# Gate and up of a gated MLP by Strassen's scheme in 11 of 14 groups, on one core

## The chip, the cores and the metric

The kernel runs on one core of a Trainium2 chip. The metric is the device time of one execution in microseconds. A run is one such time; the time before is the median of three runs. The profile is of one execution, and its span (first to last instruction) is a little shorter than a run. The engines are TensorE (PE, with its weight loads PEld), VectorE (DVE), ScalarE (ACT), GpSimd (POOL) and SyncE (SP), which issues nearly all DMAs.

## The reference

One transformer block on 2048 tokens of width 448, in float32. The first half is layer norm, 16 heads of sliding-window attention (window 256) and a residual sum. The second half is what the change is about:

```
g = layernorm(h) @ w_gate        # (2048 x 448) @ (448 x 1792)
u = layernorm(h) @ w_up          # the same shape
out = h + (gelu(g) * u) @ w_down # (2048 x 1792) @ (1792 x 448)
```

## The kernel before, in words

**Numbers.** Every large float32 operand is split in two parts of a shorter format, `hi` (rounded, on ACT, `to_hi` L352) and `lo` (the rest, mostly on DVE, `to_lo` L355). A product is hi·hi + hi·lo + lo·hi, three matmuls.

**Attention.** It runs in 16 blocks (four chunks of 512 tokens by four groups of heads). PE makes projections (L630), values (L578), scores (L680), probabilities (L755), attention sums (L793) and the output projection (L851); DVE takes the row maxima (L684), ACT the exponentials (L759), POOL the masks (L774). Layer norms are in `layer_norms` and `normalise`; those of the second half are transposed by DVE (L443) and through DRAM (L447 to L457) into `xT`.

**Feed-forward.** F = 1792 is cut into 14 tiles of 128 columns, held in groups of 3, 4, 4 and 3 (`GROUPS`); for each group the four chunks of 512 tokens are gone through. A product (`product`, L1011) is one tile by one chunk, gate and up: 56 products. K = 448 is three and a half times 128 rows. The first four products are made with full-height matmuls (L1024), 11 for gate and 11 for up. The other 52 are *paired* (`pair`, L996): the array is used as two halves of 64 rows, and gate runs in one half while up runs in the other; a second phase swaps the halves. The phases have 10 and 11 pairs of 64x512 matmuls. Between them a one-element ACT read of the bank (`seen`, L1004) makes sure that one half's writes are done before the other half writes the same bank. After a product ACT makes the gelu (L1064), DVE the product (L1066), ACT and DVE the split (L353, L356), and the down projection follows two products later: four phases of pairs of 64x448 matmuls a product, in two *down halves* of six pairs. When a group of tiles is through for a chunk, DVE adds the four banks to the residual `hres` (L1102).

**Order.** Nothing is scheduled by the compiler. The kernel records its operations with a cost, a key and their dependencies; `Lists.run` (L133) builds a fixed list for each engine from them, always taking the operation with the lowest key among those that could start first. The feed-forward's paired phases and down halves are chained one behind the other (end of `feed_forward`, L948), in the order phase, down half, phase, down half. Engines run their lists in order. Banks 0 to 3 serve gate and up, 4 to 7 down.

**Weights.** One load per tile (`weight_load`), split on ACT and DVE (`weight_splits`, the first two tiles on POOL), into seven places that are used in turn.

Of the kernel before, what the change touches and what calls it, by code (L numbers as in the profile page):

```python
# [16 lines left out]
NT = S // 128  # L17
# [7 lines left out]
GROUPS = [3, 4, 4, 3]  # L25
REC = 2944
# [8 lines left out]
LAG_T = 5.0  # L35
FETCH = 180
VLAST = (-30, -25, 14, 24)
ELAST = 2
WKEY = (256, 271)
LAG_P = 15.5  # L40
LAG_V = 9.5
EDGE = 7
WIN = 10
FFN = 1000
LEAD = 20
MARGIN = 0.7
START = 0.8
EARLY = 2
SWAP = -60
HOLDO = 1  # L50
AHEAD = 7
BEHIND = 5
LN1 = (0, -18, 55, 128)
LN2 = (158, 233)
VKEY = (-30, -23, 14, 24)
# [4 lines left out]
PAIRED = 4  # L60
TURNED = (12, 13, 14, 15)
SPANS = {"pp", "proj", "raw", "xT", "h", "rqf", "rkf", "vm", "rec0", "rec1", "rec2", "gh"}
# [167 lines left out]
def block_kernel(ctx: ExitStack, tc, x, wqk_in, wv_in, wo_in, ffn_in, out):  # L230
# [16 lines left out]
    rq_m = pool.tile([128, 4096], F32R, name="rq")  # L247
    rk_m = pool.tile([128, 6144], F32R, name="rk")
# [3 lines left out]
    mt = pool.tile([128, 768], F32, name="mt")  # L252
    xn = [pool.tile([128, D], F32, name=f"xn{i}") for i in range(2)]
# [19 lines left out]
    ffn_d = dram.tile([128, 1472], F32, name="ffn2")  # L273
    xn_d = [dram.tile([D, 128], F32, name=f"xn{t}") for t in range(NT)]
# [3 lines left out]
    fst = ExitStack()  # L278
    lp = fst.enter_context(tc.tile_pool(name="late", bufs=1))
    pp_m = lp.tile([128, 4 * PPB * 128], F32, name="pp")  # L280
# [4 lines left out]
    rec = []  # L285

    def open_rec():
        fst.close()
        p = ctx.enter_context(tc.tile_pool(name="fp", bufs=1))
        rec.extend(p.tile([128, REC], F32R, name=f"rec{i}") for i in range(2))  # L290
        rec.append(p.tile([128, S], F32R, name="xh"))
        rec.append(p.tile([128, 1024], F32R, name="gh"))


    rq = [rq_m[:, 2048 * u:2048 * u + 2048].rearrange("p (j t) -> p j t", j=4) for u in range(2)]
    rk = [rk_m[:, 3072 * u:3072 * u + 3072].rearrange("p (j t) -> p j t", j=4) for u in range(2)]
# [4 lines left out]
    ge = mt[:, 0:512]  # L301
# [39 lines left out]

    def at_v(t):
        return 7 - t % 8
# [14 lines left out]
    def dma(key, size, fn, r=(), w=(), cost=0.44, after=()):  # L358
        return op("sp", cost, 0, key, fn, r, w, size=size, after=after)
# [37 lines left out]
    def normalise(t, key, kind):  # L397
        moved = kind == "ln2" or t in TURNED
        i2, i4 = 0 if moved else t % 2, t % 4
        b = None if moved else Bank(kind)  # L400

        def norm():
            nc.scalar.activation(xn[i2], hres[:, t, :], AF.Identity, scale=bnve[:, 1, i4:i4 + 1],  # L403
                                 bias=bnve[:, 2, i4:i4 + 1])
# [20 lines left out]
        if kind == "ln1" and t in POOLED:  # L425
            op("pool", 1.0, 1.1, key, norm_pool, [HR(t), ("bnve", i4)], [("xn", i2)], port=True)
        else:
            op("act", 0.7, 0.76, key, norm, [HR(t), ("bnve", i4)], [("xn", i2)])
        if moved:
            turn(t, key, kind)  # L430
            turned(t, key, kind)
            return
        op("pe", 0.44, 0.61, key, tr, [("xn", i2), "ident"], (), b)
# [6 lines left out]
    def turn(t, key, kind):  # L440
        d = xn_d[t]
        xb, at = (v_m[:, 0:D], span("vm", 0, D)) if kind == "ln2" and t > 11 and t % 2 else (xn[1], ("xn", 1))
        op("dve", 0.56, 0.65, key, lambda: nc.vector.transpose(xb, xn[0]), [("xn", 0)], [at], port=True)  # L443
        for a in range(4):
            dst = d.rearrange("(b i) t -> i b t", i=32)[:, :, 32 * a:32 * a + 32]
            src = xb[32 * a:32 * a + 32].rearrange("i (b t) -> i b t", t=32)
            dma(key, 150, lambda dst=dst, src=src: nc.sync.dma_start(dst, src), [at], [("xnd", t, a)])  # L447

    def turned(t, key, kind):
        tc = t if kind == "ln2" else col(t)  # L450
# [830 lines left out]
```

## Time and profile before

| | us |
|---|---|
| runs: median (lowest to highest) | 719.81 (719.48 to 720.09) |
| span of the profiled execution | 718.0 |
| PE busy / PEld busy | 710.8 / 592.1 |
| DVE / ACT / POOL busy | 396.8 / 349.1 / 163.4 |

The page gives the span, not a time of its own for the profiled execution; the span is 1.8 us below the median of the runs. Attention fills the first 300 us or so, and the feed-forward runs from there to the end. In rows of groups, `out<-in` are tile names, then partitions x elements, count, busy us and mean ns of one, and the idle time before them with what ended it. Rows of a timeline have start, duration, engine, line, operation and tiles. A PE row's duration reaches to the modelled end of its last matmul, so rows overlap; pitches are read from starts.

### The profile page before, as it was taken

What the parts mean: (1) busy time and instruction counts of PE and PEld (TensorE: products, weight loads), DVE (VectorE), ACT (ScalarE), POOL (GpSimd) and SP (SyncE); (2) the same over time, 40 slices, a digit from 0 to 9 for tenths busy, and PEclk for the clock granted to TensorE, in tenths of its full rate; (3) what the DMA queues carried; (4) which work ended last, traced back from release to release, by engine and by line L of the source; (5) the groups of instructions that cost most, each with busy time, mean ns of one, the idle gap of its engine ahead of it and who ended that gap; (6) DMA issues with size and microseconds to landing.
All of it is one profiled execution on the core that took longest, in us unless ns stands there. A gap on an engine that the chain in (4) does not pass through costs nothing.

```text
span 718.0 us, 14862 instructions
## 1 busy us (share of the span) xinstructions
PE 710.8 (99%) x5716; PEld 592.1 (82%) x5716; DVE 396.8 (55%) x1034; ACT 349.1 (49%) x787; POOL 163.4 (23%) x284
## 2 busy tenths in 40 slices
PE   8999999999999999999999999999999999999997
PEld 7887778788878887778888888888888888888886
DVE  7957688988788789857544312335132235132224
ACT  7738676768667679875533222244222223222221
POOL 5604553644454466541000000000000000000000
PEclk9999999999999999999999999999999999999999
DMA  8895976787858787223641000021000000001002
GB/s 312 265 309 177 279 190 178 198 255 204 221 131 239 202 255 180 64 77 73 188 136 43 1 2 1 1 84 55 33 1 2 1 1 1 2 1 52 22 32 103
DMA packets 96926, 82.03 MB, mean 114 GB/s; under 512 B 41736, under 2 KB 83016, under 8 KB 96840
## 3 DMA queue, kind: packets, MB, share of 16 engines
q1 hardware_dynamic: 96712, 80.98, 39.5%
q8 instruction: 45, 0.74, 0.4%
q14 instruction: 25, 0.20, 0.1%
q10 hardware_dynamic: 144, 0.11, 0.0%
HBM read 50.27 MB, written 31.03 MB: 113 GB/s over the span
## 4 chain that ended last, share of the span: by engine, by line
PE 94%; ACT 2%; DVE 2%; POOL 1%; issue 1%; DMA 0%; DVEq 0%; ACTq 0%
PE bank L1000 52%; PE bank L630 10%; PE bank L755 7%; PE bank L680 6%; PE bank L793 6%; PE bank L578 5%; PE bank L851 4%; PE bank L1024 3%; PE bank L408 1%; ACT rq L353 1%; ACT xn L403 0%; DMA hres<-in_x_dram 0%; DVE hres L854 0%; DVE hres L1102 0%; PE bank L711 0%
## 5 line engine op out<-in xcount | busy, mean ns | idle before, releaser
L684 DVE CUSTOM_DVE_ANT_0 mt<-bank,mt 128x384 bf16<-128x384 f32 (+2 forms) x256 | 127.5, 527 | 33.9 <-PE bank L680 31.0
L1066 DVE TENSOR_TENSOR mt<-bank,mt 128x512 f32<-128x512 f32 x54 | 37.1, 688 | 142.2 <-ACT mt L1064 142.2
L759 ACT ACTIVATE pp<-bank 128x384 f32<-128x384 f32 (+1 forms) x212 | 103.2, 533 | 22.5 <-PE bank L755 18.3
L630 PE MATMUL bank<-xT 128*128 128x512 f32 x308 | 94.6, 397 | 0.0
L774 POOL TENSOR_SCALAR_AFFINE_SELECT pp<-pp 128x512 f32<-128x512 f32 x120 | 75.0, 640 | 67.0 <-ACT pp L759 62.7
L1064 ACT ACTIVATE mt<-bank 128x512 f32<-128x512 f32 x54 | 32.2, 596 | 117.1 <-PE bank L1000 117.1
L1000 PE MATMUL bank<-xT,rk 64*128 64x512 f32 x656 | 82.0, 388 | 0.0
L1000 PE MATMUL bank<-xT,rec 64*128 64x512 f32 x656 | 82.0, 388 | 0.0
L755 PE MATMUL bank<-rq,rk 104*128 104x384 f32 (+2 forms) x352 | 81.4, 305 | 0.4 <-ACT pp L759 0.3
L680 PE MATMUL bank<-rk,rq 84*128 84x384 f32 (+2 forms) x256 | 80.6, 340 | 0.0
L1102 DVE TENSOR_TENSOR hres<-bank,hres 128x448 f32<-128x448 f32 (+1 forms) x65 | 35.7, 611 | 67.8 <-PE bank L1000 66.0
L1000 PEld LDWEIGHTS bank<-xT,rec 64*128 64x128 f32 x656 | 63.0, 184 | 12.2
L1000 PEld LDWEIGHTS bank<-xT,rk 64*128 64x128 f32 x656 | 63.0, 184 | 12.2
L755 PEld LDWEIGHTS bank<-rq,rk 104*128 104x128 f32 x352 | 59.1, 189 | 13.7 <-ACT pp L759 3.8
L1000 PE MATMUL bank<-xT,proj 64*128 64x512 f32 x533 | 66.9, 389 | 0.4 <-ACT e L1006 0.3
L1006 ACT ACTIVATE e<-bank 1x1 f32<-1x1 f32 x162 | 25.7, 159 | 79.4 <-PE bank L1000 78.8
L630 PEld LDWEIGHTS bank<-xT 128*128 128x128 f32 x308 | 55.6, 189 | 6.2 <-ACT xT L353 0.2
L1000 PEld LDWEIGHTS bank<-xT,proj 64*128 64x128 f32 x533 | 51.0, 184 | 11.0 <-ACT e L1006 1.1
L680 PEld LDWEIGHTS bank<-rk,rq 84*128 84x128 f32 x256 | 46.8, 189 | 11.7 <-DVE mx L684 1.7
L353 ACT ACTIVATE rq<-bank 8x512 fp32r<-8x512 f32 x64 | 37.7, 589 | 27.9 <-PE bank L711 26.9
L578 PE MATMUL bank<-proj,xT 128*128 128x448 f32 (+1 forms) x220 | 47.5, 334 | 0.0
L793 PE MATMUL bank<-pp,v 128*29 128x384 f32 (+2 forms) x704 | 45.4, 388 | 0.0
(147 smaller groups left out, 1075.1 us busy)
## 6 DMA issues: line engine op xcount, KB each, us to landing
rk<-k SPq DMA_DIRECT2D x44, 336.0 KB
rq<-q SPq DMA_DIRECT2D x32, 336.0 KB
v<-in_ffn_dram SPq DMA_DIRECT2D x7, 736.0 KB
q<-proj SPq DMA_DIRECT2D x11, 448.0 KB
raw<-in_ffn_dram SPq DMA_DIRECT2D x6, 736.0 KB
xn<-xn SPq DMA_DIRECT2D x72, 56.0 KB
xT<-xn SPq DMA_DIRECT2D x20, 192.0 KB
hres<-in_x_dram SPq DMA_DIRECT2D x16, 224.0 KB
```

The lines of the kernel that those rows point to most:

```text
L353: nc.scalar.activation(dst, src, AF.Copy)
L578: op("pe", mm(224 * n), 0.29 if n == 1 else 0.38, key + a / 16, lambda a=a, h=h, wb=wb, xb=xb: nc.tensor.matmul(bank[b.k][:, 0:224 * n], x ...
L630: op("pe", mm(512) + 0.002, 0.403, key, lambda a=a, h=h, wb=wb, xb=xb: nc.tensor.matmul(bank[b.k], wqk[m][:, h, wb, :], xT[:, xb, cc * 128 ...
L680: nc.tensor.matmul(bank[b.k][:, o:384], rq[u][0:3 * DH, j, i * 128:i * 128 + 128], rk[u][0:3 * DH, j, m0 * 128:(i + 3) * 128], start=True, ...
L684: nc.vector.tensor_tensor_reduce(junk[s % 2][:, o:384], bank[b.k][:, o:384], mask[:, o:384], 1.0, -BIG, OP.add, OP.max, mx[:, i, j:j + 1])
L755: nc.tensor.matmul(bank[b.k][:, n * i:n * i + n], rk[u][0:104, j + i, m * 128:m * 128 + 128], rq[u][0:104, j + i, lo * 128:(hi + 1) * 128] ...
L759: nc.scalar.activation(pp[:, j:j + G, o * 128:o * 128 + n], bank[b.k][:, 0:G * n].rearrange("p (g t) -> p g t", g=G), AF.Exp, scale=SCALE)
L774: nc.gpsimd.affine_select(a, a, pattern=[[0, 4], [-cm, 128]], compare_op=op_, fill=0.0, base=0, channel_multiplier=cm)
L793: nc.tensor.matmul(bank[b.k][32 * j:32 * j + DH + 1, lo * 128:(hi + 1) * 128], v[:, at_v(4 * c - 2 + m), 4 * g + j, :], pp[:, j, at[m] * 1 ...
L1000: nc.tensor.matmul(bank[bk.k][:, 0:n], w, m, start=bool(start), stop=bool(stop), tile_position=(64 * x, 0), skip_group_check=True)
L1066: op("dve", 0.605, 0.702, key + 2 * NP, lambda: nc.vector.tensor_tensor(blocks(g2), src(1), blocks(g2), op=OP.mult), [*G2, *held[1]], G2, ...
L1102: nc.vector.tensor_tensor(hres[:, t, c0:c0 + w], bank[b.k][:, c0:c0 + w], hres[:, t, c0:c0 + w], op=OP.add),
```

## The change

The 14 tiles become 7 pairs of tiles and the four chunks 2 pairs of chunks: 14 groups of 256 columns by 1024 tokens, each gate and up. The order is pairs 0 to 4 with the first chunk pair, 5 and 6 with both, then 0 to 4 with the second (`ORDER2`).

- **Strassen, 11 groups.** 384 of the 448 rows are taken as two halves of 192 = 3 x 64. Columns, rows and tokens in two halves each make a 2x2 block product, done with seven products instead of eight (Winograd's form: sums of weight blocks and of token blocks are made first, and partial results are shared). The 64 rows left are added in the ordinary way. A *unit* is gate or up of a group. A *slot* is two things on the two halves of the array, three terms each: three pairs of 64x512 matmuls. Two units share 25 slots; a down half stands after every third one and at the seams, eight in all.
- **Reads in between.** Products 1, 6, 7 and 4 accumulate in one bank. After product 1 and after product 6 ACT copies the bank (`copied`), after product 7 DVE adds it to a partial result (`added`), and then the next product goes on in the same bank. A second bank is read once on its way, and a third at its end.
- **New operations.** POOL makes the weight sums (6 a weight set), DVE mostly the token sums (4 for each of three row blocks and chunk pair), ACT and DVE split both. Weights go from the input to DRAM scratch (`bounce`) and from there to SBUF, 64 rows at a time, into three buffers. Weights of pairs 3 and 4 and so on are loaded for each chunk pair where they are not used back to back.
- **First three groups, ordinary.** Pairs 0, 1, 2 with the first chunk pair are made as before in 64-row pairs (`cslot`), 28 slots a group. Group 0's operations are placed among the last blocks of attention. The full-height matmuls are gone. Layer norms of tokens 1024 to 2047 come later.
- **Last down group.** Group 13's down weights have places of their own, and its first chunk uses the banks of gate and up.
- `xn` and `v` space, banks and keys are rearranged for this; constants of the planner (`LAG_T`, `LN1`, `VKEY` and others) are set anew.

Core of the diff, with the paired product replaced:

```diff
-GROUPS = [3, 4, 4, 3]
+CL = 3
...
-    def pair(key, n, lat, a, b, r, banks):
-        def go():
-            for x, (bk, w, m, start, stop) in enumerate((a(), b())):
-                nc.tensor.matmul(bank[bk.k][:, 0:n], w, m, start=bool(start), stop=bool(stop),
-                                 tile_position=(64 * x, 0), skip_group_check=True)
-        return op("pe", mm(n), lat, key, go, r, (), banks)
...
+    PRODUCT = {1: (0, 0), 6: (0, 1), 7: (0, 2), 4: (0, 3), 2: (1, 0), 5: (1, 1), 3: (1, 2)}
...
+        order = (5, "22", 2, "11", 3, "12")
+        u.long = [(p, k, u.a) for p in (1, 6, 7, 4) for k in range(3)] + [("21", 0, u.a)]
+        u.short = []
+        for p, rest in zip(order[::2], order[1::2]):
+            b = u.b if p == 2 else u.c
+            u.short += [(p, k, b) for k in range(3)] + [(rest, 0, b)]
...
+    def both(key, *two):
...
+            for t, (wl, xl) in enumerate(((0, 0), (0, 1), (1, 0))):
+                for u, p, k, b, (side, ws, wk, xs, xk) in two:
+                    w = rest_at(wl) if ws == 4 else warea(u.w, wl, ws, side, wk, 1)
+                    nc.tensor.matmul(bank[b.k], w, xarea(u.cp, xl, xs, side)[:, xk], start=p in (1, 2, 5) and not k and not t,
+                                     stop=t == 2, tile_position=(64 * side, 0), skip_group_check=True)
+        queued(op("pe", 0.69, 0.86, key, go, reads, (), [x[3] for x in two]))
...
+    def after(key, u, p, k):
+        last = k == 2
+        if p == 1 and last:
+            copied(key, u.buf["11"], u.a)
+        elif p == 6 and last:
+            copied(key, u.buf["12"], u.a)
+        elif p == 7 and last:
+            added(key, u.buf["22"], u.a)
+            finished(key, u, "22")
+        elif p == "21":
+            finished(key, u, "21")
+        elif p == "22":
+            copied(key, u.buf["22"], u.c)
+        elif p == "11":
+            added(key, u.buf["11"], u.b)
+            finished(key, u, "11")
+        elif p == "12":
+            added(key, u.buf["12"], u.c)
+            finished(key, u, "12")
...
+            for i in range(12):
+                key = start + UNIT * i / 12.5
+                if i in (3, 6, 9):
+                    pause(key)
+                slot(key, (ua, *ua.long[i]), (ua, *ua.short[i]))
+            key = start + UNIT
+            seen(key, ua.a)
+            pause(key)
+            slot(key, (ua, *ua.long[12]), (ub, *ub.long[0]))
```

`pause` places the next waiting down half; `queued` chains a PE operation behind the one before. `weight_set` holds the weight sums, for example:

```diff
+        sum_(0, SE, 2, lambda: at(0, 1, 2), lambda: at(0, 2, 2), OP.add, wtok(n, 0, 1, 2) + wtok(n, 0, 2, 2))
+        sum_(384, SG, 2, lambda: at(0, 0, 2), lambda: at(0, 1, 2), OP.subtract, wtok(n, 0, 0, 2) + wtok(n, 0, 1, 2))
```

950 lines of the change are left out of this document (669 added, 281 removed).

## The prediction, made before the changed kernel ran

> **What bounds the kernel now.** I read the page first, for the share of TensorE and for the chain that ended last.
>
> ```profile
> span 718.0 us, 14862 instructions
> ...
> PE 710.8 (99%) x5716; PEld 592.1 (82%) x5716; DVE 396.8 (55%) x1034; ACT 349.1 (49%) x787; POOL 163.4 (23%) x284
> ...
> PE 94%; ACT 2%; DVE 2%; POOL 1%; issue 1%; DMA 0%; DVEq 0%; ACTq 0%
> ```
>
> TensorE (PE) is busy for 99% and makes 94% of the chain. A busy PE need not be a full one, so I looked next at stretches of the run, at the waits, and at the matmul pitch inside one product.
>
> ```profile
> 300.00:325.00 25.00, 24.93 (x172) 19.17 (x172) 14.56 (x28) 20.33 (x40) 8.17 (x12) 1.00 0.30 73
> 325.00:350.00 25.00, 24.74 (x216) 20.26 (x215) 16.55 (x33) 11.60 (x29) 3.21 (x8) 1.00 0.53 119
> 400.00:700.00 300.00, 300.00 (x2744) 256.96 (x2742) 92.24 (x148) 79.95 (x229) 0.00 (x0) 1.00 0.05 17
> ```
>
> The columns are the stretch, its length, busy time of PE, PEld, DVE, ACT and POOL, granted clock, DMA share and GB/s. From 400 to 700 us PE has no gap at clock 1.00, while DVE works 31% of the time, ACT 27% and POOL not at all. In the list of waits, PE's on the feed-forward's bank reads come to one row:
>
> ```profile
> PE bank L1000 <- ACT e L1006: 0.3, 1, 0.3
> ```
>
> (total, times, longest, in us). Then the pitch, from the timeline:
>
> ```profile
> 401.74 2.67 PE L1000 MATMUL bank<-xT,rk 64*128 64x512 f32 x21
> ...
> 404.03 0.39 PE L1000 MATMUL bank<-xh,rk 64*128 64x512 f32 x1
> ...
> 404.25 1.37 PE L1000 MATMUL bank<-rq,gh 64*128 64x448 f32 x12
> 404.45 0.60 ACT L1064 ACTIVATE mt<-bank 128x512 f32<-128x512 f32 x1 [2.29 <-PE bank L1000]
> ...
> 405.27 0.62 PEld L1000 LDWEIGHTS bank<-xT,rec 64*128 64x128 f32 x6
> 405.46 0.62 PE L1000 MATMUL bank<-xT,rec 64*128 64x512 f32 x4
> ```
>
> This is one phase (22 matmuls, 11 pairs on the two row halves) and one down half (12 matmuls, 6 pairs). The phase lasts from 401.74 to 404.25, so a 512-column pair costs 2.51/11 = **0.228 us**; the down half lasts to 405.46, so a 448-column pair costs 1.21/6 = 0.202 us. The bound is the number of pairs; time falls only if pairs go, and only while nothing else makes PE wait.
>
> **The change, part by part.**
>
> *Pairs removed.* The 512-column matmuls of gate and up:
>
> ```profile
> L1000 PE MATMUL bank<-xT,rk x656: 386/386/394, 391.0 to 693.1; 64*128 64x512 f32 x164
> ...
> L1000 PE MATMUL bank<-xT,rq x287: 383/386/493, 339.7 to 613.6; 64*128 64x512 f32 x144
> ```
> ```profile
> 281.95 2.91 PE L1024 MATMUL bank<-xT,proj 128*128 128x512 f32 x12
> ```
>
> These are the first and the last of four rows, 656 + 656 + 533 + 287 = 2132 = 52 products x 41; the 42nd matmul of each product reads `xh` instead of `xT`. That is 52 x 21 = 1092 pairs. Four unpaired products have 22 full-height matmuls each, 88, at the same pitch: (2.91 - 0.40 of the last one)/11 = 0.228 us. Together 1180. After: an ordinary group (256 columns by 1024 tokens, gate and up) needs 84 pairs, a Strassen group 25 slots of 3 = 75. So 3 x 84 + 11 x 75 = 1077, and the built program counts the same (504 + 1650 matmuls). All other PE instructions keep their counts. Removed: 103 x 0.228 = **23.5 us**.
>
> *Moving the first groups to attention's end.* The windows above show PE busy for 49.67 of 50 us there already, so filling gaps earns little. I take 0, bounds -3 and +3: the stretch may lose its small waits or gain new ones, as 64-row slots now wait on layer-norm results that pass through DRAM.
>
> *Reads in the middle of an accumulation.* This is the new wait. In each of 22 Strassen units one bank collects products 1, 6, 7, 4, and is read after 1 and 6 (ACT copy, 128x512) and after 7 (DVE add, 128x512) before PE may go on in it: 66 reads. One down half stands between. PE's instructions form one fixed list, so a late read stops everything behind it. What a read costs:
>
> ```profile
> L1066 DVE TENSOR_TENSOR mt<-bank,mt 128x512 f32<-128x512 f32 x54 | 37.1, 688 | 142.2 <-ACT mt L1064 142.2
> ...
> L1102 DVE TENSOR_TENSOR hres<-bank,hres 128x448 f32<-128x448 f32 x63 | 35.1, 618 | 67.8 <-PE bank L1000 66.0 <-PE bank L1093 1.8
> ...
> L1064 ACT ACTIVATE mt<-bank 128x512 f32<-128x512 f32 x54 | 32.2, 596 | 117.1 <-PE bank L1000 117.1
> ...
> L353 ACT ACTIVATE gh<-mt 128x512 fp32r<-128x512 f32 x27 | 17.0, 631 | 41.4 <-DVE mt L1066 34.3 <-PE bank L1000 7.1
> ```
> ```profile
> 358.05 0.35 ACT L1006 ACTIVATE e<-bank 1x1 f32<-1x1 f32 x2
> 358.26 0.18 PEld L1000 LDWEIGHTS bank<-xT,proj 64*128 64x128 f32 x2 [0.65 <-ACT e L1006]
> ```
>
> In the timeline at 404 us ACT began 0.03 us after the last matmul ended (404.03 + 0.39 to 404.45) and the weight load behind the down half issued at 405.27. A copy of 0.60 would end at 405.05, an add of 0.69 at 405.14. The last fence shows the hand-back: two small reads from 358.05 on take 0.35 us, so the first ends near 358.22, and PE's load follows some 0.05 us later. That leaves 0.17 us of slack for a copy and 0.08 for an add, which also queues 0.03 behind the add of another bank. So with free engines all 66 cost nothing; each is lost only by as much as ACT or DVE is late.
>
> How busy are they? From the built order times the rows, DVE in a group of 25 slots and 8 down halves (25 x 0.684 + 8 x 1.21 = 26.8 us) has six adds and four products and four splits at 0.69, eight output adds at 0.618 and weight splits: 15.7 to 21.4 us, and 25.0 and 26.1 us in groups 4 and 5 (counted from 0), where the second token half is also made. ACT, with copies at 0.60 and splits at 0.63, has 13 to 20 us. If a read met a random moment, ACT (55% busy, ops of 0.6) would lose 0.55 x 0.43^2/1.2 = 0.085 us a copy and DVE (75%, ops of 0.65) 0.75 x 0.6^2/1.3 = 0.21 us an add: 44 x 0.085 + 22 x 0.21 = 8.3 us. The lower bound is 0, the upper one a whole foreign operation ahead of every read: 44 x 0.43 + 22 x 0.61 = 32 us. The lists put reads first among what is ready, so I take half of the random figure: **4 us**.
>
> *VectorE's full stretches.* Between attention's last drain and the first Strassen add, the built order gives DVE 64 us by the rows, against 201 + 72 pairs (and 24 output-projection matmuls) = 65 us of PE. Groups 4 and 5 hold 51.1 against 53.6. And POOL, idle from 350 us on, now makes weight sums:
>
> ```profile
> L356 POOL TENSOR_TENSOR proj<-raw,proj 128x448 fp32r<-128x448 f32 x4 | 4.6, 1160 | 1.2 <-ACT proj L353 1.2
> ...
> L704 DVE SCALAR_TENSOR_TENSOR mhl<-mx,mhl 128x16 fp32r<-128x16 f32 x16 | 4.5, 283 | 0.4
> ```
> ```profile
> 284.40 1.29 POOL L356 TENSOR_TENSOR ohl<-oT,ohl 128x512 fp32r<-128x512 f32 x1 [0.77 <-ACT ohl L353]
> ...
> 284.61 1.12 DVE L704 SCALAR_TENSOR_TENSOR mhl<-mx,mhl 128x16 fp32r<-128x16 f32 x1
> ```
>
> The tiny DVE operation that averages 283 ns took 1.12 us and ended at 285.73, just after the POOL operation it met (285.69). A weight set has five sums of 384 (1160 x 384/448, about 1.0 us), one of 128 and two small splits: 6.5 us, two sets a group, so POOL is busy half of the time. Some 16 DVE operations a group read two SBUF tiles; meeting POOL half the time and waiting half an operation, they lose about 16 x 0.5 x 0.45 = 3.6 us a group. Elsewhere that fits; in the two full stretches 64 us + 11 and 51 us + 7 overrun PE by about 10 and 5. Bounds 0 and 15 us; work due late can slide into the slack around, so I take **4 us**. (The Trainium skill, "SBUF — State Buffer", section "Who interferes with whom", says that a VectorE instruction with two SBUF inputs contends with a GpSimd instruction that reads SBUF and that the loser fully blocks; the pair at 284 us agrees. It speaks against this change, and the sum without it would be 4 us lower.)
>
> *Transfers.* Each weight set moves about 2 MB (0.5 read and written, then 1.0 loaded), 4 MB in a group of 26.8 us, 150 GB/s.
>
> ```profile
> GB/s 312 265 309 177 279 190 178 198 255 204 221 131 239 202 255 180 64 77 73 188 136 43 1 2 1 1 84 55 33 1 2 1 1 1 2 1 52 22 32 103
> ```
>
> The first slices carry up to 312. A set's buffer is free for two units (26.8 us); load 5, sums 6.5, splits 4 fit. I take 0, upper bound 5 if sums wait on loads in POOL's queue. SP issues 554 instead of 366, all far from its limit. *Tail:* the same 15 cut matmuls and stores: 0.
>
> **Sum.** 718.0 - 23.5 + 0 + 4 + 4 + 0 + 0 = 702.5 us of span. The median of the runs, 719.81, lies 1.8 us above the span, so **704.3 us**.
>
> **Rivals.**
> *Nothing given back.* If reads and stretches are all covered and the move gains a little, 719.8 - 23.5 and up to 1 less: 695 to 697. For it: PE waited 0.3 us in all where before has the same pattern, a read behind a down half. Against: those reads take 0.16 us and DVE idles.
> *VectorE becomes the bound in its two full stretches.* The overruns of 10 and 5 us come in whole: 719.8 - 23.5 + 4 + 15 = 715. For it: the 284 us pair, 98% demand. Against: slack in the groups beside.
> *Slower: every read in mid-accumulation is queued behind another operation.* Place: the three points of each unit where one bank goes on. Price up to 32 us: 719.8 - 23.5 + 32 = 728. It decides from 23.5/66 = 0.36 us a read on. For it: ACT splits that wait for DVE stand directly ahead of copies in ACT's order. Against: it needs a full foreign operation each time on engines 50 to 75% busy. (The Trainium skill, "TensorEngine Tiling (Array Packing)", section "PSUM Bottleneck", warns that tiling speeds up TensorE but not the evacuation; no run here shows it yet, and it would end as this rival.)
> *It does not do what it says* (a Strassen slot of two different products runs below a pair's pitch): against it, the pairs of before also use two banks and two weights. At 0.24 a pair, 825 x 0.012 = 10 us back: 714.
>
> **How the numbers follow.** Forecast case (698 to 711) 0.62; nothing given back 0.08; VectorE's stretches (711 to 718) 0.15; slots below pitch 0.03; reads queued, 718 and up, 0.12, of which a fourth stays near 719.8. The range 695 to 715 leaves out the slower case and the upper end of VectorE's. About 0.2% (1.4 us) is what a measurement of this kernel can tell from no change. Faster 0.87, same 0.04, slower 0.09.
>
> **What would show it.** Right: 504 + 1650 matmuls of 64x512 at 0.228 us a pair; groups of about 27 us; PE's waits on the ACT copies and DVE adds a few us in sum, largest in groups 4 and 5; DVE over 90% busy from attention's end to the first Strassen unit. Wrong: waits at those reads over 0.3 us each; PE waiting for weights or for DMA; a lower granted clock.

## The result, and the profile after

The changed kernel takes **713.92 us** (median; 713.54 to 714.32) where the one before takes 719.85 us on the same chip: ratio **0.9918, 95% interval 0.9904 to 0.9932**. The forecast was 704.3 us. The sign was right and 713.9 lies inside the range, but of the forecast gain of 15.5 us only 5.9 came.

From the page of the changed kernel, its span and the busy times:

```profile
span 712.4 us, 15568 instructions
...
PE 698.2 (98%) x5598; PEld 589.1 (83%) x5598; DVE 536.8 (75%) x1233; ACT 415.9 (58%) x917; POOL 312.7 (44%) x426
```

PE still has no slack in its share, so the page doesn't say where the rest went. Stretches of the two runs do. First the kernel before, then the changed one (start:end, length, busy PE, PEld, DVE, ACT, POOL, clock, DMA share, GB/s):

```profile
270.00:330.00 60.00, 59.71 (x422) 46.40 (x416) 47.49 (x127) 47.59 (x101) 30.45 (x49) 1.00 0.42 101
330.00:520.00 190.00, 189.65 (x1728) 161.51 (x1728) 71.54 (x121) 63.60 (x173) 3.02 (x8) 1.00 0.19 56
520.00:690.00 170.00, 170.00 (x1558) 145.63 (x1555) 53.31 (x85) 44.47 (x127) 0.00 (x0) 1.00 0.03 12
```
```profile
270.00:330.00 60.00, 58.77 (x443) 40.16 (x444) 40.57 (x114) 43.60 (x89) 26.83 (x45) 1.00 0.28 75
330.00:520.00 190.00, 184.51 (x1650) 158.10 (x1647) 148.84 (x235) 99.25 (x250) 85.94 (x84) 1.00 0.57 158
520.00:690.00 170.00, 170.00 (x1550) 157.73 (x1548) 121.13 (x181) 82.89 (x205) 71.90 (x72) 1.00 0.35 107
```

PE stands still for 5.5 us between 330 and 520, where VectorE works 78% of the time, and not at all from 520 on, where it works 71%. Between 270 and 330 us, at attention's end, VectorE and ACT work *less* than before, and PE's weight loads have shrunk from 46.4 to 40.2 us. The waits of the weight loads for exponentials (ACT) and maxima (VectorE) there, before and after (total, times, longest):

```profile
PEld bank L755 <- ACT pp L759: 1.4, 5, 0.5
...
PEld bank L680 <- DVE mx L684: 0.6, 1, 0.6
```
```profile
PEld bank L792 <- ACT pp L796: 4.5, 12, 0.7
PEld bank L717 <- DVE mx L721: 3.3, 6, 0.9
```

These waits have grown from 2.0 to 7.8 us. But weight loads run ahead of the matmuls, and the matmuls themselves stand still for only 1.2 us of the 60 (60.00 less 58.77), 0.3 before. So these waits can be only a small part of the loss.

**An account of PE's time.** To add this up I split each run at the last output-projection matmul:

```profile
323.83 2.80 PE L851 MATMUL bank<-proj,ohl 128*128 128x448 f32 x13
```
```profile
326.67 2.85 PE L888 MATMUL bank<-proj,ohl 128*128 128x448 f32 x13
```

The rows (before, then after) end at 326.63 and 329.52; the last matmul in them starts 0.37 us earlier, and there attention ends. Each feed-forward matmul in the PE records is counted at its pitch (0.2275 us a pair or full-height matmul of 512 columns, 0.2015 of 448). *Ahead* is the time of that last matmul less the feed-forward work done by then; *behind* is the time from there to the last PE start less the work left.

| kernel | last output matmul | feed-forward work by then | ahead | work in all | behind |
|---|---|---|---|---|---|
| before | 326.27 | 20.02 | 306.25 | 403.9 | 3.86 |
| after | 329.15 | 16.38 | 312.77 | 380.5 | 14.26 |

Work: -23.4 us, as forecast. Ahead: **+6.5 us**. Behind: **+10.4 us**. After PE's end there is 0.9 us more. Together -5.6 us, the difference of the spans (718.0 and 712.4).

**What the 6.5 us ahead are made of.** The starts of the matmuls show it. First the changed kernel, where a burst of three 64-row pairs (L1123) stands between attention's matmuls; then the kernel before, where single full-height matmuls (L1024) stand there:

```profile
270.88 0.40 PE L792 MATMUL bank<-rq,rk 104*128 104x256 f32 x2
271.20 0.96 PE L1123 MATMUL bank<-xT,proj 64*128 64x512 f32 x6
272.10 0.44 PE L717 MATMUL bank<-rk,rq 84*128 84x384 f32 x1
272.37 0.40 PE L792 MATMUL bank<-rq,rk 104*128 104x256 f32 x2
```
```profile
271.24 0.34 PE L680 MATMUL bank<-rk,rq 84*128 84x384 f32 x1
271.42 0.40 PE L1024 MATMUL bank<-xT,proj 128*128 128x512 f32 x1
271.65 0.40 PE L755 MATMUL bank<-rq,rk 104*128 104x256 f32 x2
271.89 0.39 PE L1024 MATMUL bank<-xT,proj 128*128 128x512 f32 x1
```

The three pairs take 0.90 us (271.20 to 272.10) in place of 0.68. The two matmuls ahead of them take 0.32 in place of the 0.24 that such a two take before (271.65 to 271.89), and the one behind 0.27 in place of 0.18 (271.24 to 271.42). So a burst costs about 0.4 us beyond its pitch. All twelve bursts of three pairs take 0.89 or 0.90. Fifteen bursts stand ahead of the last output matmul; counted from the starts they cost 6.0 us in all. In the kernel before no change of row height stands ahead of its last output matmul. Three waits of PE add 1.8 us by the same count, before none.

### The profile page after: what moved, and what is told of

Its sections match the earlier page's. It is cut to its first block, busy times and chain, and to the rows that moved or that the text cites. A ratio compares the mean times of both kernels' runs of the same rounds, so it can differ in the third digit from the quotient of the medians.

```text
span 712.4 us, 15568 instructions
## 1 busy us (share of the span) xinstructions
PE 698.2 (98%) x5598; PEld 589.1 (83%) x5598; DVE 536.8 (75%) x1233; ACT 415.9 (58%) x917; POOL 312.7 (44%) x426
## 5 line engine op out<-in xcount | busy, mean ns | idle before, releaser
L811 POOL TENSOR_SCALAR_AFFINE_SELECT pp<-pp 128x512 f32<-128x512 f32 x120 | 77.2, 658 | 86.1 <-ACT pp L796 83.8
L1314 PE MATMUL bank<-xT,proj 64*128 64x512 f32 x735 | 95.2, 388 | 0.0
L1314 PEld LDWEIGHTS bank<-xT,proj 64*128 64x128 f32 x735 | 77.7, 184 | 7.1 <-ACT raw L1320 0.2
L1388 PE MATMUL bank<-proj,gh 64*128 64x448 f32 x624 | 72.9, 363 | 2.0 <-ACT e L1234 2.0
L1388 PEld LDWEIGHTS bank<-proj,gh 64*128 64x128 f32 x624 | 61.7, 184 | 7.4 <-ACT e L1234 2.7
L1405 DVE TENSOR_TENSOR hres<-bank,hres 128x448 f32<-128x448 f32 (+1 forms) x113 | 62.9, 611 | 6.4 <-PE bank L1388 6.4
L1234 ACT ACTIVATE e<-bank 1x1 f32<-1x1 f32 x145 | 22.8, 157 | 68.0 <-PE bank L1388 48.0
L1183 POOL TENSOR_TENSOR xn<-proj 128x384 f32<-128x384 f32 (+1 forms) x36 | 37.2, 1039 | 56.6 <-DMA proj<-gu 42.9
L1123 PE MATMUL bank<-xT,proj 64*128 64x512 f32 x420 | 53.5, 396 | 0.0
L1314 PE MATMUL bank<-xo,proj 64*128 64x512 f32 x366 | 48.5, 390 | 2.9 <-DVE v L1324 1.9
L387 DVE TENSOR_TENSOR proj<-proj 128x448 fp32r<-128x448 f32 (+2 forms) x42 | 31.0, 743 | 25.0 <-ACT proj L384 22.8
L1123 PEld LDWEIGHTS bank<-xT,proj 64*128 64x128 f32 x420 | 38.2, 184 | 10.4 <-issue 2.6
```

Source lines behind the costliest of these rows:

```text
L811: nc.gpsimd.affine_select(a, a, pattern=[[0, 4], [-cm, 128]], compare_op=op_, fill=0.0, base=0, channel_multiplier=cm)
L1123: nc.tensor.matmul(bank[banks[side ^ ph].k], cwbuf[n % 4][0]()[HALF[side], o:o + 128], carea(c, xl, j, side), start=not ph and not j and n ...
L1314: nc.tensor.matmul(bank[b.k], w, xarea(u.cp, xl, xs, side)[:, xk], start=p in (1, 2, 5) and not k and not t, stop=t == 2, tile_position=(6 ...
L1388: nc.tensor.matmul(bank[banks[q].k][:, 0:D], h[oh][0]()[HALF[x], q * 128:q * 128 + 128], d[wh][0]()[HALF[x]], start=not ph and not y and n ...
L1405: op("dve", 0.07 + w * 0.463 / D, 0.163 + w * 0.463 / D, key, lambda: nc.vector.tensor_tensor(hres[:, t, c0:c0 + w], bank[b.k][:, c0:c0 + ...
```

## The experiments

Theory at the start: three places give the time back, attention's end (6.5), single late reads between 330 and 515 us (about 7) and the last group (about 2). Rivals: each read in the middle of an accumulation has a price of its own (A); POOL against VectorE is everything (B). What a burst costs at its ends was in the theory only in part, as 0.108 us a burst. The ratios below are to the kernel before, with 95% intervals; the changed kernel's is 0.9918 [0.9904, 0.9932]. *Ahead* and *behind* are from one profile each; the two profiles of one kernel, full0 and full0_look, differ by about 1 us in both.

| run | us | ratio | ahead | behind |
|---|---|---|---|---|
| sums_memset | 710.57 | 0.9873 [0.9859, 0.9888] | 313.23 | 10.81 |
| reads_1x1 | 711.62 | 0.9887 [0.9871, 0.9904] | 312.72 | 11.08 |
| both | 709.01 | 0.9850 [0.9834, 0.9867] | 312.71 | 9.07 |
| tokens_1x1 | 714.48 | 0.9919 [0.9904, 0.9934] | 312.95 | 15.06 |
| late_1x1 | 713.59 | 0.9915 [0.9899, 0.9932] | 312.49 | 13.47 |
| prep_1x1 | 713.99 | 0.9919 [0.9904, 0.9934] | 312.54 | 14.61 |
| full0 | 714.23 | 0.9923 [0.9908, 0.9938] | 305.91 | 20.49 |
| full0_look | 715.56 | one run | 307.05 | 21.45 |
| no_fill / before_no_fill | 733.11 / 740.51 | one run each | 327.02 / 328.42 | 19.05 / 2.42 |
| refill | 715.57 | 0.9938 [0.9926, 0.9951] | 307.11 | 21.15 |
| refill_pieces | 712.93 | 0.9907 [0.9894, 0.9921] | 306.21 | 19.95 |
| refill2 | 715.19 | 0.9942 [0.9927, 0.9958] | 307.64 | 20.11 |
| after_light | 708.31 | 0.9840 [0.9824, 0.9856] | 312.79 | 8.32 |
| full0_light | 707.43 | 0.9827 [0.9813, 0.9842] | 305.76 | 14.19 |
| pieces | 716.54 | 0.9952 [0.9938, 0.9965] | 312.98 | 16.40 |
| halves_same | 714.70 | 0.9930 [0.9916, 0.9944] | 313.03 | 14.38 |
| thirds_same | 721.28 | 1.0015 [1.0005, 1.0024] | 312.79 | 21.75 |

### POOL's sums and the reads

**sums_memset**

```diff
-            arith("pool", w, key + 1, lambda e: e.tensor_tensor(xn_m[HALF[side], o:o + w], a(), b(), op=what), rd, [tok])
+            arith("pool", w, key + 1, lambda e: e.memset(xn_m[HALF[side], o:o + w], 0.0), rd, [tok])
```

> POOL's six weight sums per weight set are replaced by fills of the same places (nothing of SBUF is read for them; the sums are left out). The order on every engine stays. Theory (three places: attention's end gives back about 6.5 us, late reads between 330 and 511 us about 7, the last group about 2): the four waits at 404.7, 426.4, 455.3 and 511.1 us (1.19 + 1.11 + 1.34 + 0.66 = 4.3 us), each behind a VectorE operation that a POOL sum lengthened to 1.4 to 1.5 us, go for the most part: 2.5 to 4 us faster than the changed kernel, about 710 to 711.5; the splits L387 from SBUF fall from 0.86 to 0.69 us. Rival A (each read in the middle of an accumulation costs about 0.2 us by itself): no change, 714. Rival B (POOL against VectorE is the whole of what was given back): 8 us or more faster, 706 or less.

710.57 us, 3.35 less: as the theory said. The intervals of the two ratios don't meet. What happened to VectorE is in the groups of its operations, of the changed kernel and of sums_memset (count, busy us, mean ns, idle before):

```profile
L1324 DVE TENSOR_TENSOR v<-bank,v 128x512 f32<-128x512 f32 x33 | 22.4, 688 | 12.3 <-PE bank L1314 11.9
L387 DVE TENSOR_TENSOR gh<-v,gh 128x512 fp32r<-128x512 f32 x26 | 22.4, 862 | 5.1 <-ACT gh L384 5.0
...
L387 DVE TENSOR_TENSOR e<-v,e 128x512 fp32r<-128x512 f32 x13 | 11.5, 887 | 3.9 <-ACT e L384 3.7
```
```profile
L1324 DVE TENSOR_TENSOR v<-bank,v 128x512 f32<-128x512 f32 x33 | 22.6, 691 | 22.3 <-PE bank L1314 22.1
L387 DVE TENSOR_TENSOR gh<-v,gh 128x512 fp32r<-128x512 f32 x26 | 17.9, 688 | 6.0 <-ACT gh L384 5.9
...
L387 DVE TENSOR_TENSOR e<-v,e 128x512 fp32r<-128x512 f32 x13 | 8.9, 688 | 4.5 <-ACT e L384 4.2
```

Two SBUF inputs: 862 and 887 ns beside POOL's sums, 688 beside fills. One input from a bank: 688 and 691, untouched. (By the Trainium skill, "SBUF — State Buffer", section "Who interferes with whom", a VectorE instruction with two SBUF inputs contends with a GpSimd instruction that reads SBUF and not with one that only writes it. The trace agrees with both halves, 862 against 688.)

How 0.8 us on VectorE becomes a wait of PE is in the timeline, of the changed kernel and then of sums_memset:

```profile
402.31 2.53 POOL L1183 TENSOR_TENSOR xn<-xn,proj 64x384 f32<-64x384 f32 x2
...
403.60 1.51 PE L1388 MATMUL bank<-proj,gh 64*128 64x448 f32 x12
...
403.88 1.51 DVE L387 TENSOR_TENSOR xT<-e,xT 128x512 fp32r<-128x512 f32 x1
...
405.49 0.60 ACT L1320 ACTIVATE e<-bank 128x512 f32<-128x512 f32 x1 [0.95 <-DVE xT L387]
405.98 0.34 ACT L1234 ACTIVATE e<-bank 1x1 f32<-1x1 f32 x2
406.13 0.73 PE L1314 MATMUL bank<-xo,proj 64*128 64x512 f32 x4 [1.02 <-ACT e L1234]
```
```profile
404.02 0.69 DVE L387 TENSOR_TENSOR xT<-e,xT 128x512 fp32r<-128x512 f32 x1
...
404.80 0.60 ACT L1320 ACTIVATE e<-bank 128x512 f32<-128x512 f32 x1
405.29 0.33 ACT L1234 ACTIVATE e<-bank 1x1 f32<-1x1 f32 x2
405.45 0.73 PE L1314 MATMUL bank<-xo,proj 64*128 64x512 f32 x4 [0.20 <-ACT e L1234]
```

The ACT copy of the bank writes the buffer `e`, which VectorE's split still reads; that split meets a POOL sum and takes 1.51 us in place of 0.69. The copy, the one-element reads behind it and PE move by the same 0.8 us, counted from the start of the down half (403.60, and 403.75 in sums_memset). PE's step here, the time between the starts of two pairs beyond the pitch, is 1.19 us in the changed kernel and 0.38 without the sums. Those near 426, 455 and 511 us shrink from 1.11, 1.34 and 0.66 to 0.33, 0.51 and 0.11. (At 455 us the two halves of the array run 0.2 us apart, and the step is counted from the one that ends first; from the other it is 1.14 and 0.32.)

**reads_1x1** (copies and adds of a bank on one element) and **both** (with the fills):

```diff
+        n = (1, 1) if buf[1] in whole else (128, 512)
+        whole.add(buf[1])
...
-        op("act", 0.49, 0.605, key, lambda: nc.scalar.activation(buf[0](), bank[b.k], AF.Copy), gate_of(buf), [buf[1]], b)
+        op("act", 0.49, 0.605, key, lambda: nc.scalar.activation(buf[0]()[0:n[0], 0:n[1]], bank[b.k][0:n[0], 0:n[1]], AF.Copy),
+           gate_of(buf), [buf[1]], b)
...
-        op("dve", 0.605, 0.702, key, lambda: nc.vector.tensor_tensor(buf[0](), bank[b.k], buf[0](), op=OP.add),
+        op("dve", 0.605, 0.702, key, lambda: nc.vector.tensor_tensor(
+            buf[0]()[0:1, 0:1], bank[b.k][0:1, 0:1], buf[0]()[0:1, 0:1], op=OP.add),
```

> In the Strassen units the ACT copies and VectorE adds of a bank in the middle or at the end of an accumulation read and write one element in place of 128x512 (a buffer's first copy stays whole); the partial results are left out. The order on every engine stays. Theory (three places): only the late reads of 400 to 511 us and small change go, 3 to 5 us: 709 to 711. Rival A (the reads themselves are the price, 0.2 us each and more): 11 to 15 us faster, 699 to 703. Rival B (POOL against VectorE): 1 to 3 us faster, since the splits it lengthens stay.

> The two edits of sums_memset and reads_1x1 together (weight sums and partial results left out, the same order). If the reads are late because POOL lengthens VectorE's operations, the two gains of 3.4 and 2.3 us are largely the same microseconds: 709.5 to 710.5. Rival A (reads have a price of their own beside POOL): they add up, 708 to 708.5 or less.

The reads give 2.3 us, less than the theory's 3 to 5 and far less than rival A's 11 to 15. Together the edits give 4.9 us: 709.01 lies between the two expectations, 1.56 us beyond sums_memset, a little more than "largely the same microseconds" and less than the full sum of 5.65. So A has at most a small part of its own, about 1.6 us for 66 reads. Rival B fails: the sums are worth 3.35 us of the 17.6 that were given back (23.5 less 5.9).

**tokens_1x1** tests whether VectorE is simply full, **late_1x1** two waits in the ordinary groups:

```diff
-                scratch(1, 0), f(area(1, 2, k, 0)), f(area(1, 1, k, 0)), op=OP.subtract),
+                cut(scratch(1, 0)), cut(f(area(1, 2, k, 0))), cut(f(area(1, 1, k, 0))), op=OP.subtract),
```

(`cut` takes one element; in the one kernel of the second half's token operations, in the other of the weight splits of group 2.)

> VectorE's and POOL's sums and low parts of the second token half (27 operations of 128x512 or half of it, between 390 and 480 us) work on one element; these operands are left out. The order on every engine stays, and so do POOL's weight sums. Theory (single reads come late behind one VectorE operation that POOL lengthened): of the five waits between 400 and 515 us only those that stand behind such a token operation go, 1 to 2.5 us: 711.5 to 713. Rival F (VectorE is simply full, up to 95% busy between 450 and 480 us): nearly all waits between 390 and 480 us go, 5 to 6 us: 708 to 709.

> ACT's and VectorE's splits of the weights of group 2 (eight operations of 128x448 between 345 and 385 us) work on one element; these operands are left out. The order stays. Theory (the waits of 1.09 us at 349.9 and 1.19 us at 380.4 us come from such a split standing between two ACT copies of banks): both shrink to 0.3 to 0.6 us, 1 to 2 us faster: 712 to 713. Rival: the two copies behind each other need more than one down half of PE work (1.21 us) anyway, and the waits stay: 714.

Both missed. Without 27 VectorE and POOL operations there is no gain; of the waits named only the one near 455 us shrank (1.34 to 0.80), and 511 grew from 0.66 to 1.09. The wait at 405 us stays at 1.19, because the split in front of it is of a product of group 2 and no token operation. VectorE being full (rival F, 708 to 709 us) is not the cause; but my own count of 1 to 2.5 us was wrong too. In late_1x1 the wait near 350 us fell from 1.09 to 0.34, as said; the one near 380 stayed (1.19 to 1.16), so another split stands there: `w<-xn`, which itself waits for a POOL sum (0.62 in sums_memset). In the median nothing can be told from the changed kernel.

### Attention's end

**no_fill, before_no_fill**: no banks for the feed-forward until the output projection is through.

```diff
-            return [] if left["proj"] or left["v"] else [5 + kind[1]]
+            return [] if left["att"] or left["task"] else [5 + kind[1]]
...
```

> The changed kernel, but gate and up of group 0 get no banks until attention's last output projection is through, so nothing of the feed-forward stands among attention's blocks. Theory (attention's last blocks are paced by maxima, exponentials and masks, and leave PE about 20 us of gaps that the feed-forward fills): the last output-projection matmul stays near 329 us (325 to 330) though 16.4 us of PE work are gone from ahead of it, and the whole takes 12 to 18 us longer: 726 to 732. Rival D (PE paces attention's end, so what is put there costs its own time): the last output-projection matmul comes at about 313 and the whole stays at 714.

> The kernel before with the same edit: its unpaired products get no banks until attention's last output projection is through. Theory: the last output-projection matmul stays near 326 us (322 to 327) without the 20 us of filler, so that the two kernels leave nearly the same gaps and the one before had put 3.6 us more into them; the whole takes 15 to 20 us longer: 735 to 740. Rival D: 306 us, and 720 for the whole. Rival E (attention itself is slower after the change, by the new places of its operations): this kernel's last output-projection matmul is 3 us or more ahead of that of no_fill.

```profile
324.68 2.71 PE L888 MATMUL bank<-proj,ohl 128*128 128x448 f32 x12
```
```profile
325.76 3.02 PE L851 MATMUL bank<-proj,ohl 128*128 128x448 f32 x11
```

Without any filler the last output matmul starts at 327.0 us (changed) and 328.4 us (before): 16.4 us of work gone from ahead of it bring it forward by only 2.1 us, and without its 20.0 us the kernel before gets there 2.1 us later, not earlier. The totals are a little above what was expected (733.1 against 726 to 732, 740.5 against 735 to 740). Rival E falls: the changed kernel's attention is not the later one. Rival D's figures (313 and 306 us, no change in the whole) didn't come either, but these runs don't show that attention's end is paced by other engines, because the granted clock fell in them:

```profile
270.00:280.00 10.00, 9.40 (x44) 7.07 (x47) 8.68 (x32) 6.59 (x14) 7.21 (x16) 0.69 0.41 105
...
290.00:300.00 10.00, 9.86 (x53) 7.05 (x54) 8.74 (x24) 6.99 (x17) 6.60 (x10) 0.66 0.00 0
```

Over the rows of 10 us of no_fill from 270 us on the mean clock is 0.69, 0.97, 0.66, 0.89 and 0.77, then 0.76 up to 327. So about 12 us of work at full clock were lost to the clock, and only 6.7 us of these 57 are idle time of PE. In the two rows shown PE is busy for 94% and 99% at two thirds of the clock. What is shown: without filler PE waits for other engines and runs slower, and the filler's time is hardly won back. How much of a gap there would be at full clock stays open; the 20 us of the theory are not shown.

**full0, full0_look** (one kernel, run twice):

```diff
+            for i in range(2):
+                for j in range(3):
+                    for t, (wl, xl) in enumerate(((0, 0), (0, 1), (1, 0))):
+                        o = 384 * i + 128 * j
+                        op("pe", mm(512) + 0.002, 0.403, key + 4 * i + j + t / 3, lambda i=i, j=j, t=t, wl=wl, xl=xl, o=o: nc.tensor.matmul(
+                            bank[banks[i].k], cwbuf[n % 4][0]()[:, 896 * (1 - wl) + o:896 * (1 - wl) + o + 128], carea(c, xl, j, 2),
+                            start=not j and not t, stop=False, skip_group_check=True),
+                           [*cwtok(n, wl, o, 128, 2), *ctok(c, xl, j, 2)], (), banks[i])
+            cslot(key + 9, n, c, 1, 3, banks)
...
```

> The first three turns of group 0, those that fill attention's last blocks, are made with 18 full-height matmuls and three pairs of 64 rows each, recorded one by one and not chained, in place of seven chained slots of three pairs: the same 21 steps of 0.2275 us. Theory (the filler at attention's end is coarse and its bursts begin with 0.108 us lost, so it no longer fits the gaps): the last output-projection matmul comes at 326 to 327 us in place of 329.2; of that up to 3 us can be lost again before group 2, whose weights come no earlier, so 711 to 714 in all. Rival C (ACT's and VectorE's preparation of group 0 holds attention's blocks up): the last output-projection matmul stays at 329, 714.

> full0 once more, for its stages: the first three turns of group 0 in full-height single matmuls. Theory: more filler fits, 20 us of feed-forward work ahead of the last output-projection matmul in place of 16.4, and PE's progress at 330 us is 2 to 3 us ahead of the changed kernel; a wait of 3 us or more ahead of group 2, whose weights come due at a fixed time, takes it back. Rival: the progress at 330 us is the same.

The same 21 steps, but 18 of them as single full-height matmuls outside the chain and not as 64-row slots of 0.68 us. The last output matmul comes at 325.70 and 326.84 us in the two profiles (329.15 in the changed kernel), with 19.8 us of feed-forward work ahead of it and not 16.4, and the clock at 1.00. *Ahead* goes from 312.8 to **307.05** (305.91 in the other profile): 5.7 us or all of the 6.5 that were lost. The filler's form is the cause at this place. Its changes of row height explain most of it: four bursts are left in full0_look, which cost 1.5 us by the same count and not 6.0 (2.0 in the other profile). Full0 also makes the filler finer and takes it out of the chain; what these two are worth by themselves is not separated, and 1 to 3 us are left for them. And it changes nothing in the total: *behind* goes from 14.3 to 21.5 us.

**prep_1x1** (the preparation of the ordinary groups on one element):

> ACT's and VectorE's splits of the tokens and of the first three weight sets of the ordinary groups, done during attention's last blocks, work on one element (these operands are left out). The order on every engine stays. Theory (coarse filler): attention's end moves by at most 1 us, 713 to 714. Rival C (this preparation is what makes PE wait for maxima and exponentials): the last output-projection matmul comes 3 us or more earlier, 711 or less.

713.99 us, the total of the changed kernel, and the last output matmul comes at 328.92 us, 0.2 us earlier and not 3 or more. Rival C falls: the preparation does not hold attention's blocks up.

### What takes it back

**refill, refill2, refill_pieces**: more full-height turns (nine, five and nine in place of full0's three), and the keys and lags from which the kernel builds its lists set anew for them; refill_pieces also cuts the sums.

> full0 (here with the first nine turns of the ordinary groups in full-height matmuls) and new keys and lags, so that the weights and tokens of the next groups come as much earlier as PE does: the kernel's own order is written anew. Theory (the 6.5 us at attention's end and part of the late reads are a matter of the order and of the filler's form, not of the scheme): attention's end keeps full0's gain of about 5.7 us and the loss behind it stays at 10 to 15 us: 706 to 711. Rival H (whatever is gained at attention's end is lost again behind it, since VectorE, ACT and the DMAs must be through with the same work): 713 to 715.

> Another order of the same kind, with five full-height turns and 1.6 us more filler ahead of attention's last output projection. Theory: as refill, 706 to 711. Rival H: 713 to 715.

> refill with the sums in pieces of 128 columns. Theory: 1 to 2 us less than refill. Rival G: the same as refill or slower.

All three keep 5.1 to 6.6 us at attention's end, and all three lose as much behind it. The sum of ahead and behind is 327.0 in the changed kernel, 328.5 in full0, 328.3, 327.8 and 326.2 in these. That looked like rival H: work due behind attention's end that PE must wait for. **after_light** and **full0_light** tell it apart: the edits of both, most token operations of VectorE and the splits of group 2 taken away, in the two orders.

> The edits of both, and besides most of the token sums and low parts of the Strassen groups (33 VectorE and POOL operations of about 60) and the weight splits of group 2 on one element: these operands are left out. The order stays that of the changed kernel. Theory: not much under both, which took the lengthening and the reads away already, 707 to 709; attention's end stays at 329 us.

> The same edits in the order of full0. Rival H (what full0 gains at attention's end is lost again behind it because VectorE's, ACT's and POOL's preparation is due there): with most of that work gone the gain of 5.7 us survives, 702 to 704, and the loss behind attention's end is 8 to 10 us as in both. Rival I (the loss behind goes by the order, by hand-overs and by transfers, not by the amount of work): the loss behind stays above 13 us, 707 us or more, no better than after_light.

Behind is 8.3 us in the one order and 14.2 in the other, with the same light load: rival H falls as it was put, though not all of that work was taken away, and the difference of 5.9 us is the order's. The largest wait of full0, 2.53 us near 369 us, is 2.53 us in full0_light as well, where VectorE works 46% of these 15 us:

```profile
360.00:375.00 15.00, 12.52 (x97) 9.75 (x95) 6.83 (x16) 6.64 (x18) 1.42 (x2) 0.89 0.87 205
```
```profile
364.96 2.60 PE L1401 MATMUL bank<-proj,e 64*128 64x448 f32 x24
...
367.07 2.22 DVE L1418 TENSOR_TENSOR hres<-bank,hres 128x448 f32<-128x448 f32 x4 [1.56 <-PE bank L1401]
...
369.20 1.28 DVE L1159 TENSOR_TENSOR v<-bank,v 128x512 f32<-128x512 f32 x2
```

VectorE idles 1.56 us for PE's down halves, then makes four output adds, and only then the product L1159 that frees the bank for which PE waits. VectorE goes through a fixed list, and the product stands behind the adds in it. Behind this wait the clock is 0.72 from 370 to 376 us, which is another 1.7 us. So this one place holds some 4.2 of the 5.9 us.

**pieces, halves_same, thirds_same**: each sum in pieces, in pieces with a new order, in the other two with the order kept.

```diff
+            def go(e):
+                for c in range(0, w, 128):
+                    n = min(128, w - c)
+                    e.tensor_tensor(xn_m[HALF[side], o + c:o + c + n], a()[:, c:c + n], b()[:, c:c + n], op=what)
```

> The changed kernel with each POOL weight sum of 384 columns cut in three of 128 (nothing left out; POOL's time goes up, as 64x128 takes 0.47 and 64x384 about 1.0 us alone). Theory (a VectorE operation that reads two SBUF tiles loses what POOL's instruction has still to run): a VectorE operation then loses at most 0.4 to 0.5 us in place of up to 0.8, and a third to a half of the 3.4 us of sums_memset comes back: 711.5 to 713. Rival G (the loss goes by POOL's total time on the port, not by the length of one instruction): no gain, 714 to 715.

> The same with two pieces of 192 columns. Theory: between the changed kernel and thirds_same, 712.5 to 713.5. Rival G: 714 to 715.

> The sums in pieces of 128 columns as in pieces, but the order of the changed kernel kept on every engine (three POOL instructions stand where one stood; nothing left out). Theory (what a VectorE operation loses goes by the length of the one POOL instruction it meets): the splits gh<-v fall from 0.862 to about 0.75 us, the waits near 405, 426, 455 and 511 us shrink by a third or more, 711.5 to 713. Rival G (by POOL's total time): 714 to 716; POOL's later ends push the weight splits back.

The theory predicted a gain. There is a loss against the changed kernel: 2.6 us for pieces, 7.4 for thirds_same, none to tell for halves_same. Rival G's 714 to 715 fits halves_same alone; the other two are above both. In part the theory was right: in thirds_same the splits `gh<-v` fall to 799 ns, and the waits near 405, 427 and 455 us to 0.64, 0.40 and 0.49. But the wait near 511 us grows from 0.66 to 1.54. And POOL needs longer for a set, weight splits wait for its sums, and ACT's bank reads stand behind those splits: the step near 380 us grows from 1.19 to 2.68 us. PE's waits in thirds_same:

```profile
PE bank L1392 <- ACT e L1238: 4.5, 3, 2.5
PE bank L1318 <- DVE v L1328: 2.6, 4, 1.4
```

In the changed kernel these two rows are 2.0 and 2.4 us. POOL, busy for 49% of the span (44% in the changed kernel), stands on the path through ACT's list.

No kernel here that computes the whole beats the changed one: refill_pieces, 0.9907 against 0.9918, can't be told from it.

## Why the prediction was right in sign and wrong in size

- **Pairs removed: right.** 504 and 1650 matmuls of 64x512 are in the trace; the work fell by 23.4 us (23.5 forecast). A pair of a Strassen slot goes at the old pitch: in the timeline of the changed kernel 18 matmuls take from 684.03 to 686.07, 0.227 us a pair. The rival of slower slots is out.

```profile
684.03 2.26 PE L1314 MATMUL bank<-xT,proj 64*128 64x512 f32 x18
...
686.07 1.44 PE L1388 MATMUL bank<-proj,gh 64*128 64x448 f32 x12
```

- **"Moving the first groups to attention's end": this step failed.** I took 0 with bounds of 3 us; it cost 6.5. I read "PE busy for 49.67 of 50 us" as no gaps to fill and asked only whether the new filler would wait. But 20.0 us of that busy time were single feed-forward matmuls of attention's own height. The change put 16.4 us of 64-row slots there, in 15 bursts, and each burst costs about 0.4 us at the changes of row height, 6.0 us in all. The form was left out of the sum. full0 wins 5.7 us back with full-height filler. The reasons I gave for the bounds, DRAM and layer norms, play no part in PE's waits there. The sum failed in a second way: it adds its terms, but what full0 wins ahead of attention's end is lost behind it, so the term is not worth 6.5 us in the total as long as the order behind stays.
- **Reads in the middle of an accumulation: size nearly right.** 4 us forecast, 2.3 measured (1.6 beside sums_memset). The rival of all reads queued is out.
- **VectorE's full stretches: size right, mechanism half.** 4 us forecast; POOL's sums cost 3.35 us, and the lengthening is as derived. But not by an overrun of VectorE's total. The forecast had 75 us of work (64 and 11 by POOL) between attention's last output matmuls and the first Strassen add, and 58 in groups 4 and 5. VectorE's busy time in these stretches is 52.7 us of 72.2 and 51.7 of 57.6:

```profile
324.30:396.50 72.20, 70.19 (x604) 58.80 (x604) 52.68 (x93) 38.10 (x96) 20.54 (x23) 1.00 0.71 184
416.80:474.40 57.60, 55.62 (x496) 48.15 (x494) 51.71 (x76) 33.92 (x81) 34.35 (x31) 1.00 0.50 148
```

  The sign that was named, over 90% up to the first Strassen unit, did not come (73%), and taking work off VectorE gave nothing (tokens_1x1). One lengthened operation ahead of one read does it. That the size came out is luck, and so is the 715 us of the rival "VectorE becomes the bound": it came close for a reason that didn't hold.
- **Tail: wrong.** I took 0. Behind 680 us PE loses 1.9 us (before 0.4), and 0.9 us is added after its end. The rows of before and after:

```profile
711.53 2.75 PE L1093 MATMUL bank<-rec,gh 128*128 128x448 f32 x15
712.51 2.49 DVE L1102 TENSOR_TENSOR hres<-bank,hres 128x448 f32<-128x448 f32 x5 [1.76 <-PE bank L1093]
...
714.74 0.37 ACTq L1109 DMA_DIRECT2D out_dram<-hres  x1
```
```profile
704.57 4.41 DVE L1405 TENSOR_TENSOR hres<-bank,hres 128x448 f32<-128x448 f32 x9 [4.58 <-PE bank L1388]
...
705.00 2.77 PE L1421 MATMUL bank<-w,xT 128*128 128x448 f32 x15
...
708.71 0.37 ACTq L1411 DMA_DIRECT2D out_dram<-hres  x1
```

  In the new order of the last down group nine output adds stand together and not five, so the last ones come late: the last store issues 0.94 us after PE's end, before 0.46. The other 0.4 us after PE's end were not taken apart.
- **Transfers: 0 was right**, as far as PE's waits go: none of those quoted ends on a DMA.
- **What is left open.** Behind attention's end 10.4 us were added. By the profiles 3.45 of them go with the sums, 1.74 more with the reads and 0.75 more with token operations and splits; the last is less than two profiles of one kernel differ by. 1.5 belong to the last group. The other 3 us are small waits that I didn't take apart. Whether an order exists that keeps both ends is open; those measured do not.

## What to carry to other kernels

A busy engine may be busy with filler: before work is moved, find what stands in its new place, and compare the form of the new filler with its neighbours, for the changes between forms can cost more than the gaps. Where engines run fixed lists, time saved at one place is lost at the next hand-over unless the lists behind it move too, so account for PE by stages and not only by the total. And a change that loads an idle engine should be followed to the engine whose list waits for its result.

## What the runs showed of the hardware

- A short wait of PE can cost more than itself. After the wait of 2.4 to 2.5 us in full0_look, the mean clock granted was 0.57 for 3 us and 0.86 for the next 3, some 1.7 us of full-clock work lost; after the same wait in full0_light it was 0.72 for 6 us, the same 1.7 us:

```profile
370.00:373.00 3.00, 0.64 (x3) 0.33 (x5) 3.00 (x7) 2.10 (x5) 2.92 (x5) 1.00 0.81 169
373.00:376.00 3.00, 3.00 (x18) 2.34 (x20) 2.98 (x3) 0.00 (x0) 1.76 (x2) 0.57 0.69 176
```

  (The Trainium skill, "TensorE: Matmul & The Clock Gate", section "Why this matters for your kernels", advises against PE gaps above about 3 us; here gaps of 2.4 to 2.5 us already went ahead of a lower clock.) Waits of 1.1 to 1.3 us in the changed kernel left the clock at 1.00. But in no_fill, with little work between the waits, it was 0.69 from 270 to 280 us, where no wait is longer than 0.25 us. So the length of a single wait does not decide it alone.
- Changing between full-height matmuls and pairs of 64 rows cost about 0.4 us a burst at attention's end: 0.11 on the first pair, 0.10 on the step from the last pair to the next matmul, and 0.08 to 0.1 on each neighbour. A first pair after a wait loses the same 0.11.
- A POOL fill that only writes SBUF didn't lengthen VectorE's operations with two SBUF inputs (688 ns); a POOL sum did (862).
